# Second layer's first product by Strassen's algorithm, on two sets of tokens, in a three-stage float32 kernel

## The chip, the core and the metric

The kernel runs on one core of a Trainium2 chip. The metric is the time of one execution on the device in microseconds (us). The profile comes from one such execution. PE is TensorE, DVE VectorE, ACT ScalarE, POOL GpSimd, and SP issues the DMAs.

## The reference

```python
# attention without a score matrix: 4 batches x 8 heads, 576 tokens, 64 columns
q_s = exp(q - max(q)) / (sum + 1e-9)          # over a head's 64 columns
k_s = exp(k - max(k)) / (sum + 1e-9)          # over the 576 tokens
x = q_s @ (k_s^T @ v)                         # -> 2304 tokens x 512
# first layer, 2048 hidden units
h = x @ w_in
x = (h * clip(h + 3, 0, 6) / 6) @ w_out
# second layer, 4 experts of 1024 hidden units
for e in range(4):
    out += p[:, e:e+1] * (max(x @ w1[e], 0) @ w2[e])     # p normalised over e
```

All inputs are float32; the first layer's weights are taken in through the 64 bits of doubles.

## The kernel before

A product x @ w is made of float32r halves: x = H + L, and H.H + H.L + L.H are summed in PSUM. So each product of 128 x 128 weights with some columns is three matmuls.

Attention comes first, batch by batch: `k_part`, `q_part` and `x_part`, which leaves x transposed (hidden units on partitions) as `xh` and `xl`. The first layer's weights are converted on DVE, ACT and POOL meanwhile (`w_half`, lines 455 to 492), half a chunk at a time.

Both layers work by steps (`h_part`, `y_part`): a chunk of 128 hidden units for a block of tokens. A step is 12 matmuls of the first product (lines 514 to 516: four parts of 128 inputs, three halves each), the nonlinearity with the split into `gh` and `gl`, and 12 matmuls of the second product (line 590). The first layer has 16 chunks in five passes over its six blocks of 256 to 448 tokens (`PASSES1`); after a pass a block's sum is evicted into `acc`, and after the last it is halved again into `xh` and `xl` (lines 637 and 639). The second layer has 32 chunks, four to a pass, over four blocks of 512 tokens and one of 256. Its nonlinearity is a Relu on ACT out of PSUM (line 559) and the rest `gl` on DVE, which reads PSUM once and SBUF once (line 562). Its second product has tokens on partitions, so each of its matmuls has 512 columns, and the eviction (line 650) weighs it with the expert's share.

The order of all engines' instructions is set by `Plan.order`, a list schedule with a table of costs and places (`w`: weight chunks, 6 and 2 more after the attention; `g`, `ph`, `r`). Each engine then works through its list in order, and only semaphores time it.

Of the kernel before, what the change touches and what calls it, by code (L numbers as in the profile page):

```python
# [22 lines left out]
E = 4  # L23
# [22 lines left out]

# the first load's start, and until when the tensor engine runs at half its clock
FIRST, COLD = 1.65, 30.0


def hop(a, b):
    """From the end of a part on one engine to the start of one that waits for it on another."""
    return 0.27 if b == "PE" else 0.2 if a == "PE" else 1.05 if a == "SP" else 0.16


class Op:
# [3 lines left out]
    __slots__ = ("eng", "fn", "deps", "key", "take", "give", "start", "end", "place", "on", "n",  # L60
                 "left", "at", "then", "due")
# [698 lines left out]
```

## Time and profile before

| | us |
|---|---|
| median of 3 runs | 1307.83 |
| lowest, highest | 1307.62, 1310.25 |
| the profiled execution, its span | 1307.6 |
| PE busy in it | 1268.7 |
| DVE, ACT, POOL busy | 503.2, 360.8, 248.0 |

The span runs from the first to the last instruction. A matmul's shown duration reaches over its successors, so PE's spacing is read from start times. "Idle before" is an engine's idle time in front of a group, with what ended it.

### The profile page before, as it was taken

The page shows a single profiled execution, that of the slowest core. Times are in us where ns is not written, and L with a number is a line of the kernel's source. Part 1 is how long each engine was busy: PE and PEld are TensorE (multiplying, and loading weights), DVE is VectorE, ACT ScalarE, POOL GpSimd, SP SyncE. Part 2 cuts the span into 40 slices and gives each one's busy share as a digit, 9 for nine tenths or more (in the row PEclk, how much of TensorE's full clock was granted, in tenths as well). Part 3 has the DMA queues.
Part 4 walks back from the last instruction along what each step waited for, and adds up shares of the span by engine and source line. Part 5 has one row for each costly group of instructions (what it writes and reads, how often), then busy time and mean ns, then how long its engine had stood idle before and what let it go on. Part 6 is the DMA issues. An engine that isn't in the chain of part 4 may idle for free.

```text
span 1307.6 us, 15363 instructions
## 1 busy us (share of the span) xinstructions
PE 1268.7 (97%) x6336; PEld 1101.3 (84%) x6336; DVE 503.2 (38%) x849; ACT 360.8 (28%) x680; POOL 248.0 (19%) x207
## 2 busy tenths in 40 slices
PE   4889999999999999999999999999999999999998
PEld 3778999899999999888888888888888888888887
DVE  8998641884345332222222222122222222222222
ACT  5676533552234334012112112102112112111111
POOL 4665132430005215003003003003003003000000
PEclk9998999999999999999999999999999999999999
DMA  8444120231003002002002002002001001000011
GB/s 283 120 136 124 48 66 1 65 98 33 1 1 97 1 1 65 1 1 65 1 1 65 1 1 65 1 1 65 1 1 63 3 1 33 1 1 1 33 45 68
DMA packets 19254, 54.02 MB, mean 41 GB/s; under 512 B 2288, under 2 KB 2288, under 8 KB 19184
## 3 DMA queue, kind: packets, MB, share of 16 engines
q1 hardware_dynamic: 19184, 53.04, 12.9%
q8 instruction: 50, 0.82, 0.3%
q14 instruction: 20, 0.16, 0.0%
HBM read 48.31 MB, written 4.72 MB: 41 GB/s over the span
## 4 chain that ended last, share of the span: by engine, by line
PE 76%; issue 11%; DVE 5%; POOL 3%; DMA 3%; ACT 1%; SPq 0%; DVEq 0%; POOLq 0%; ACTq 0%
PE y L590 37%; PE ph L514 12%; PE ph L516 12%; PE ph L515 12%; DMA raw<-in_w_dram 2%; POOL wt L468 1%; POOL wl L436 1%; DVE wt L476 1%; PE pa L407 1%; DVE raw L485 1%; DVE wt L471 1%; PE pa L310 0%; DVE qm L381 0%; DVE raw L479 0%; PE pa L303 0%
## 5 line engine op out<-in xcount | busy, mean ns | idle before, releaser
L514 PE MATMUL ph<-xh,wh 128*128 128x512 f32 (+4 forms) x1024 | 368.4, 360 | 0.5 <-ACT xh L414 0.5
L516 PE MATMUL ph<-xh,wl 128*128 128x512 f32 (+4 forms) x1024 | 366.1, 358 | 0.0
L515 PE MATMUL ph<-xl,wh 128*128 128x512 f32 (+4 forms) x1024 | 365.3, 357 | 0.8 <-DVE xl L416 0.7
L562 DVE SCALAR_TENSOR_TENSOR gl<-ph,gh 128x512 fp32r<-128x512 f32 (+1 forms) x160 | 102.1, 638 | 568.9 <-ACT gh L559 568.9
L559 ACT ACTIVATE gh<-ph 128x512 fp32r<-128x512 f32 (+1 forms) x160 | 89.2, 557 | 641.9 <-PE ph L516 615.3
L590 PE MATMUL y<-wh,gh 128*128 128x512 f32 x576 | 227.3, 395 | 0.0
L590 PE MATMUL y<-wl,gh 128*128 128x512 f32 x576 | 226.2, 393 | 0.0
L515 PEld LDWEIGHTS ph<-xl,wh 128*128 128x128 f32 x1024 | 192.8, 188 | 26.1 <-DVE xl L416 1.4
L514 PEld LDWEIGHTS ph<-xh,wh 128*128 128x128 f32 x1024 | 192.9, 188 | 25.3 <-ACT xh L414 1.5
L516 PEld LDWEIGHTS ph<-xh,wl 128*128 128x128 f32 x1024 | 192.8, 188 | 24.6
L436 POOL TENSOR_TENSOR wl<-raw,wh 128x512 fp32r<-128x512 f32 x64 | 81.5, 1294 | 539.0 <-ACT wh L449 538.9
L590 PE MATMUL y<-wh,gl 128*128 128x512 f32 x576 | 157.9, 391 | 0.0
L590 PE MATMUL y<-gh,wh 128*128 128x448 f32 (+3 forms) x384 | 132.8, 352 | 3.9 <-ACT gh L545 3.2
L590 PEld LDWEIGHTS y<-wh,gl 128*128 128x128 f32 x576 | 108.2, 188 | 25.4
L590 PEld LDWEIGHTS y<-wl,gh 128*128 128x128 f32 x576 | 108.0, 187 | 23.5
L590 PEld LDWEIGHTS y<-wh,gh 128*128 128x128 f32 x576 | 108.2, 188 | 23.0
L590 PE MATMUL y<-gh,wl 128*128 128x448 f32 (+3 forms) x384 | 127.5, 338 | 0.0
L539 DVE SCALAR_TENSOR_TENSOR r<-r,ph 128x448 f32<-128x448 f32 (+3 forms) x96 | 52.9, 551 | 140.8 <-ACT r L536 140.6
L650 DVE SCALAR_TENSOR_TENSOR acc<-y,pt,acc 128x512 f32<-128x512 f32 x126 | 86.2, 745 | 26.4 <-PE y L590 26.4
L536 ACT ACTIVATE r<-ph,three 128x448 f32<-128x448 f32 (+3 forms) x96 | 55.4, 577 | 134.4 <-PE ph L516 133.4
L590 PE MATMUL y<-gl,wh 128*128 128x448 f32 (+3 forms) x384 | 86.9, 344 | 0.0
L590 PEld LDWEIGHTS y<-gh,wh 128*128 128x128 f32 x384 | 72.6, 189 | 9.2 <-ACT gh L545 5.0
(85 smaller groups left out, 949.3 us busy)
## 6 DMA issues: line engine op xcount, KB each, us to landing
raw<-in_w_dram SPq DMA_DIRECT2D x62, 512.0 KB, 3.7
acc<-in_kt_dram SPq DMA_DIRECT2D x16, 288.0 KB, 3.8
out_dram<-acc SPq DMA_DIRECT2D x18, 256.0 KB, 2.1
vs<-in_v_dram SPq DMA_DIRECT2D x12, 322.5 KB, 4.3
qs<-in_q_dram SPq DMA_DIRECT2D x13, 256.0 KB, 3.7
acc<-in_v_dram SPq DMA_DIRECT2D x4, 322.5 KB, 5.5
acc<-in_w_dram SPq DMA_DIRECT2D x2, 512.0 KB, 7.6
acc<-in_q_dram SPq DMA_DIRECT2D x3, 256.0 KB, 3.9
```

Source lines behind the costliest of these rows:

```text
L407: nc.tensor.matmul(ps[o], lhsT=bd[j], rhs=qt[:, j, s0:s0 + n], start=True, stop=True)
L436: on(o).tensor_tensor(out=wl[c][:, cols], in0=x, in1=wh[c][:, cols].bitcast(F32), op=ALU.subtract)
L468: on(o).tensor_tensor(out=t(F32), in0=word(1, F32), in1=t(F32), op=ALU.mult)
L514: nc.tensor.matmul(ps[0], lhsT=hi, rhs=a, start=(k == 0), stop=False)
L515: nc.tensor.matmul(ps[0], lhsT=hi, rhs=b, start=False, stop=False)
L516: nc.tensor.matmul(ps[0], lhsT=lo, rhs=a, start=False, stop=(k == NK - 1))
L536: nc.scalar.activation(out=ps["r"], in_=ps[0], func=AF.Relu, bias=three)
L539: nc.vector.scalar_tensor_tensor(out=ps["r"], in0=ps["r"], scalar=6.0, in1=ps[0], op0=ALU.min, op1=ALU.mult)
L559: nc.scalar.activation(out=s["g"][0], in_=ps[0], func=AF.Relu)
L562: nc.vector.scalar_tensor_tensor(out=s["g"][1], in0=ps[0], scalar=0.0, in1=s["g"][0].bitcast(F32), op0=ALU.max, op1=ALU.subtract)
L590: nc.tensor.matmul(y, lhsT=l, rhs=r, start=(s["start"] and not low and m == 0), stop=(s["stop"] and bool(low)))
L650: o1 = add({"DVE": 0.62}, lambda o: nc.vector.scalar_tensor_tensor(out=a, in0=ybank[b], scalar=g, in1=a, op0=ALU.mult, op1=ALU.add), [made ...
```

## The change

**The second layer's first product** takes two chunks (a pair, 256 hidden units) and a unit of tokens at once. The units (`UNITS`) are 512, 512, 512 and 768 tokens, each cut into two halves of n = 256, 256, 256 and 384. Hidden units, inputs and tokens are each split in two, and Strassen's algorithm in Winograd's form makes the four blocks from seven products of half size instead of eight. Each product is 6 matmuls of n columns, 42 a round where there were 48. Products 6, 4 and 3 accumulate in the bank of 1, 7 and 5 after ACT has evicted these; DVE and POOL add up the blocks, ACT and DVE halve them into g (`h_ops`).

**x and the weights are formed as sums and differences.** `x_forms` makes seven operands of a unit out of `acc` and halves each. `w_first` does the same for the pair's weights, on POOL, DVE and ACT.

**Two sets of tokens.** Set 0 is units 0 and 1, set 1 units 2 and 3; all 16 pairs go over set 0 first. In set 0 each formed weight is stored to DRAM (`wd`, `vd`), in set 1 it is loaded from there. Pairs go in groups of two; the second product of a group (`y_ops`) runs as a head of two tiles, and the others lie between the products of the next round.

**The first layer** goes over blocks of 256 and 384 tokens, in passes of 3, 3, 6, 5 and 5 chunks. Weight places are now 24 and 2 more of 512 columns (half a chunk's H or L).

```diff
-# (first token, tokens) of the blocks that a pass over some hidden units goes through
-BLOCKS1 = [(0, 256), (256, 320), (576, 448), (1024, 448), (1472, 416), (1888, 416)]
-BLOCKS2 = [(0, 512), (512, 512), (1024, 512), (1536, 512), (2048, 256)]
-# (chunks from, to, blocks), one after the other
-PASSES1 = [(0, 3, (0, 1, 2)), (3, 6, (0, 1, 2)), (0, 6, (3, 4, 5)),
-           (6, 12, range(6)), (12, 16, range(6))]
+BLOCKS1 = [(0, 256), (256, 256), (512, 256), (768, 256), (1024, 256), (1280, 256), (1536, 384),
+           (1920, 384)]
+PASSES1 = [(0, 3, range(4)), (3, 6, range(4)), (0, 6, range(4, 8)), (6, 11, range(8)),
+           (11, 16, range(8))]
...
+UNITS = [(0, 256), (512, 256), (1024, 256), (1536, 384)]
+BLOCKS = [(0, 1), (2, 3)]
+HALVES = ((0, 0), (0, 1), (1, 0), (1, 1))
+FORM = {(0, 0): 1, (0, 1): 2, (1, 1): 4, (1, 0): 7}
+ORDER = (1, 7, 5, 6, 4, 3, 2)
+BANK = {1: 0, 6: 0, 7: 1, 4: 1, 5: 2, 3: 2, 2: 3}
+NPE = F2 // (2 * P)
+NW, NG, NT_ = 24, 2, 3
+MORE_W, MORE_G, MORE_T = 2, 4, 5
...
-    xl = big.tile([P, NK, NT], F32R, name="xl")
+    big, xp, wp, gp, tp, wsp = (pool(x) for x in ("big", "xp", "wp", "gp", "tp", "wsp"))
+    dram = pool("dram", space=bass.MemoryType.DRAM)
...
+        def summed(i, a, b, op):
+            def make(o):
+                o.place_tile = XT[o.place] if late_ else g_tile(o.place, F32)
+                tt(o, vals[i](), vals[a](), vals[b](), op)
+            o = temps[i] = add(either(2 * n), make, ready[a] + ready[b],
...
+        got = {}
+        if blk:
+            for i in ORDER:
+                pl = w_new(w1, (pr, i))
+                ld = load("sp", {"SP": 0.9}, lambda o, i=i: nc.sync.dma_start(
+                    out=w1[pr, i].bitcast(F32), in_=wd[pr, i - 1]), [pl, w_stored[pr, i]])
+                got[i] = ld, pl, []
+            return got
+        p0, p1 = [raw2(2 * pr + f, 0) for f in range(2)]
...
+        def form(i):
+            pl = w_new(w1, (pr, i))
+            o1 = add({"ACT": act(half)}, lambda o: nc.scalar.activation(
+                out=w1[pr, i][:, :half], in_=vals[i](), func=AF.Copy), ready[i] + [pl])
+            give = [("wtmp", temps[i])] if i in temps else []
+            o2 = add(rather_pool(half), lambda o: half_sub(
+                o, w1[pr, i][:, half:], vals[i](), w1[pr, i][:, :half]),
+                [o1] + (readers[i] if i in temps else []), None, give)
+            st = add({"SP": 0.9}, lambda o: nc.sync.dma_start(
+                out=wd[pr, i - 1], in_=w1[pr, i].bitcast(F32)), [o2])
+            w_stored[pr, i] = st
+            lows[i] = o2
...
+        def product(o, i):
+            (xh, xl), ww = xf[u, i], w1[pr, i]
+            opens = i in (1, 7, 5, 2)
+            for k in range(2):
+                hi, lo = ww[:, k * P:(k + 1) * P], ww[:, (2 + k) * P:(3 + k) * P]
+                a, b = xh[:, k * n:(k + 1) * n], xl[:, k * n:(k + 1) * n]
+                for m, (l, r) in enumerate(((hi, a), (lo, a), (hi, b))):
+                    nc.tensor.matmul(
+                        bank(i), lhsT=l, rhs=r, start=(opens and k == 0 and m == 0),
+                        stop=(k == 1 and m == 2), skip_group_check=not opens)
...
+        def evict(i):
+            def f(o, t):
+                nc.scalar.activation(out=t, in_=bank(i), func=AF.Copy)
+            return tmp({"ACT": act(n)}, f, [ops[i]])
...
+        def make(i):
+            deps = [weights[i][0], xf["op", (u, i)]]
+            deps += bank_free.get(BANK[i], [])
...
+                    o, y0.place_tile[:, :n], y0.place_tile[:, :n], u2.place_tile[:, :n], ALU.add),
+                    [s, u2])
+                blocks[1, 1] = y0, [pos["c22"]]
+            if i == 4:
+                u2 = pos["u2"]
+                c = tmp({"DVE": dve(n)}, lambda o, t: tt(
+                    o, t, bank(4), u2.place_tile[:, :n], ALU.add), [ops[4], u2])
+                bank_free[1] = [c]
+                pos["c21"] = c
...
+                add({"": 0.0}, lambda o: None, [c, pos["c21"], pos["c22"]], None, [("t", u2)])
+            if i == 2:
+                a0 = pos["a0"]
+                c = add({"DVE": dve(n)}, lambda o: tt(
+                    o, a0.place_tile[:, :n], bank(2), a0.place_tile[:, :n], ALU.add), [ops[2], a0])
...
+            def low(o):
+                g = made[key][0]
+                nc.vector.scalar_tensor_tensor(
+                    out=g[:, n:2 * n], in0=x(), scalar=0.0, in1=g[:, :n].bitcast(F32),
+                    op0=ALU.max, op1=ALU.subtract)
...
+        head = [part(0, 0, None), part(1, 0, None), part(0, 1, 0), part(1, 1, 0),
+                part(0, 1, 1), part(1, 1, 1)]
...
+                for x, pr in enumerate(group):
+                    make, made = h_ops(pr, u, weights[pr], step["last"])
+                    todo = [lambda i=i: make(i) for i in ORDER]
+                    while todo or (x == 0 and tail):
+                        if todo:
+                            todo.pop(0)()
+                        if x == 0:
...
+                head, rest = y_ops(u, group, gs, seconds, step)
+                for f in head:
+                    f()
+                tail = rest
```

On PE a step of the second layer before, here a part of one with `ph` the first product's bank and `y` the second's:

```order
L514 MATMUL ph1_117<-xh_82,wh23_4504 128x512
L590 MATMUL y0_5120<-wh22_4467,gh_5155 128x512
L590 MATMUL y0_5120<-wl22_4468,gh_5155 128x512
L590 MATMUL y1_5126<-wh22_4467,gh_5155 128x512
L590 MATMUL y1_5126<-wl22_4468,gh_5155 128x512
```

And after the change, the seven products of one round (`ps0` to `ps3` are their banks, `ps4` the second product's):

```order
L878 MATMUL ps0_111<-x010_4173,w_15_1_8364 128x256 x6
L878 MATMUL ps1_112<-x070_4318,w_15_7_8376 128x256 x6
L878 MATMUL ps2_113<-x050_4332,w_15_5_8389 128x256 x6
L878 MATMUL ps0_111<-x060_4340,w_15_6_8402 128x256 x6
L878 MATMUL ps1_112<-x040_4358,w_15_4_8415 128x256 x6
L878 MATMUL ps2_113<-x030_4401,w_15_3_8428 128x256 x6
L878 MATMUL ps3_114<-x020_4425,w_15_2_8440 128x256 x6
L1001 MATMUL ps4_115<-w_14_0_0_8452,g_8665 128x512
```

Twelve wide matmuls into one bank have become seven groups of six into four banks, and three banks are taken twice within a round.

On DVE, the second layer before had a rest per step and a block's evictions:

```order
L562 SCALAR_TENSOR_TENSOR gl_5424<-ph2_1594,gh_5423 128x512
L562 SCALAR_TENSOR_TENSOR gl_5452<-ph1_117,gh_5451 128x512
L650 SCALAR_TENSOR_TENSOR acc_84<-y0_5361,pt_85,acc_84 128x512
L650 SCALAR_TENSOR_TENSOR acc_84<-y1_5367,pt_85,acc_84 128x512
L650 SCALAR_TENSOR_TENSOR acc_84<-y2_5371,pt_85,acc_84 128x512
```

Now a round in set 0 stands there so (line 294 adds, 963 makes the rests; `t` and `g` lie in SBUF):

```order
L294 TENSOR_TENSOR t_7741<-t_7741,t_7750 128x256
L294 TENSOR_TENSOR t_7741<-t_7741,t_7761 128x256
L294 TENSOR_TENSOR t_7772<-ps1_112,t_7761 128x256
L294 TENSOR_TENSOR t_7784<-ps2_113,t_7761 128x256
L963 SCALAR_TENSOR_TENSOR g_7781<-t_7741,g_7781 128x256
L294 TENSOR_TENSOR t_7728<-ps3_114,t_7728 128x256
L963 SCALAR_TENSOR_TENSOR g_7786<-t_7772,g_7786 128x256
L963 SCALAR_TENSOR_TENSOR gx1_5245<-t_7784,gx1_5245 128x256
L963 SCALAR_TENSOR_TENSOR gx1_5245<-t_7728,gx1_5245 128x256
```

One operation per step has become nine per round, six of them with both operands in SBUF.

On DVE at the first gate (539) of the fourth pass, in block 0, the kernel before had these rows (436 is the last step of a weight's conversion, 471 and 476 are a short and a long one):

```order
L436 TENSOR_TENSOR wl10_2232<-wt1_115,wh10_2231 128x512
L539 SCALAR_TENSOR_TENSOR r_2325<-r_2325,ph0_116 128x256
L471 TENSOR_SCALAR wt0_114<-raw0_112 128x512
L548 TENSOR_TENSOR gl_2336<-r_2325,gh_2335 128x256
L630 TENSOR_SCALAR acc_84<-y0_2110 128x416
L630 TENSOR_SCALAR acc_84<-y2_2118 128x416
L476 SCALAR_TENSOR_TENSOR wt0_114<-raw0_112,wt0_114 128x512
```

After the change the same place (gate 615, short step 543, long step 549):

```order
L615 SCALAR_TENSOR_TENSOR r_2517<-r_2517,ps0_111 128x256
L294 TENSOR_TENSOR w_8_1_1_2424<-st0_109,w_8_1_0_2423 128x512
L682 TENSOR_SCALAR acc_81<-ps4_115 128x384
L682 TENSOR_SCALAR acc_81<-ps6_117 128x384
L294 TENSOR_TENSOR g_2533<-r_2517,g_2533 128x256
L543 TENSOR_SCALAR st0_109<-st1_110 128x512
L615 SCALAR_TENSOR_TENSOR r_2563<-r_2563,ps2_113 128x256
L543 TENSOR_SCALAR st1_110<-st0_109 128x512
L294 TENSOR_TENSOR g_2590<-r_2563,g_2590 128x256
L549 SCALAR_TENSOR_TENSOR st0_109<-st1_110,st0_109 128x512
```

Half of chunk 10 was in place before that gate; now the second half of chunk 8 comes behind it, and chunks 9 and 10 between the later gates.

## Rows read from the trace of the kernel before

**Rows 1.** The page's head and its line on PE (busy us, share of the span, instructions).
```profile
span 1307.6 us, 15363 instructions
PE 1268.7 (97%) x6336; PEld 1101.3 (84%) x6336; DVE 503.2 (38%) x849; ACT 360.8 (28%) x680; POOL 248.0 (19%) x207
```

**Rows 2.** Stretches: us; busy of PE, PEld, DVE, ACT, POOL; granted clock; DMA share; GB/s.
```profile
30.00:65.00 35.00, 30.29 (x184) 25.77 (x185) 34.12 (x67) 24.39 (x56) 24.48 (x21) 0.89 0.44 130
600.00:700.00 100.00, 100.00 (x459) 82.50 (x458) 24.90 (x38) 16.05 (x29) 10.48 (x9) 1.00 0.07 22
```

**Rows 3.** PE in order of time: start us, us, line, operation; 512 columns, then 256.
```profile
519.43 0.40 PE L514 MATMUL ph<-xh,wh 128*128 128x512 f32 x1
547.09 0.40 PE L514 MATMUL ph<-xh,wh 128*128 128x512 f32 x1
...
117.64 0.28 PE L514 MATMUL ph<-xh,wh 128*128 128x256 f32 x1
118.94 0.28 PE L516 MATMUL ph<-xh,wl 128*128 128x256 f32 x1
```

**Rows 4.** The same view, first and last of a run: 320, 448, 416 columns.
```profile
126.23 0.31 PE L514 MATMUL ph<-xh,wh 128*128 128x320 f32 x1
127.84 0.31 PE L516 MATMUL ph<-xh,wl 128*128 128x320 f32 x1
...
146.27 0.36 PE L514 MATMUL ph<-xh,wh 128*128 128x448 f32 x1
147.67 0.36 PE L515 MATMUL ph<-xl,wh 128*128 128x448 f32 x1
...
485.37 0.35 PE L514 MATMUL ph<-xh,wh 128*128 128x416 f32 x1
494.37 0.35 PE L514 MATMUL ph<-xh,wh 128*128 128x416 f32 x1
```

**Rows 5.** Groups of DVE instructions by shape: busy us, mean ns, idle before.
```profile
L562 DVE SCALAR_TENSOR_TENSOR gl<-ph,gh 128x512 fp32r<-128x512 f32 x128 | 88.5, 692 | 505.7 <-ACT gh L559 505.7
L562 DVE SCALAR_TENSOR_TENSOR gl<-ph,gh 128x256 fp32r<-128x256 f32 x32 | 13.5, 423 | 63.3 <-ACT gh L559 63.3
L650 DVE SCALAR_TENSOR_TENSOR acc<-y,pt,acc 128x512 f32<-128x512 f32 x126 | 86.2, 745 | 26.4 <-PE y L590 26.4
L476 DVE SCALAR_TENSOR_TENSOR wt<-raw,wt 128x512 int32<-128x512 int32 x30 | 28.3, 943 | 1.5 <-ACT wt L474 1.2
L471 DVE TENSOR_SCALAR wt<-raw 128x512 int32<-128x512 int32 x30 | 16.9, 575 | 8.2 <-DMA raw<-in_w_dram 7.5 <-POOL wl L436 0.6
L436 DVE TENSOR_TENSOR wl<-wt,wh 128x512 fp32r<-128x512 f32 x12 | 16.3, 1356 | 4.7 <-ACT wh L489 4.2 <-PE y L590 0.5
```

**Rows 6.** Groups of ACT and of POOL instructions by shape, the same columns.
```profile
L559 ACT ACTIVATE gh<-ph 128x256 fp32r<-128x256 f32 x32 | 12.3, 384 | 71.3 <-PE ph L516 44.7 <-DVE acc L650 26.5
...
L639 POOL TENSOR_TENSOR xl<-acc,xh 128x256 fp32r<-128x256 f32 x4 | 3.1, 802 | 9.9 <-ACT xh L637 9.9
```

**Rows 7.** All engines in order of time near the end: a product's end to ACT.
```profile
1300.55 0.39 PE L590 MATMUL y<-wh,gh 128*128 128x512 f32 x1
1300.75 0.38 ACT L559 ACTIVATE gh<-ph 128x256 fp32r<-128x256 f32 x1 [2.42 <-PE ph L516]
```

**Rows 8.** All engines in order of time around 248 us.
```profile
247.28 0.69 DVE L485 SCALAR_TENSOR_TENSOR raw<-raw 128x512 f32<-128x512 uint32 x1
248.05 1.29 POOL L468 TENSOR_TENSOR wt<-raw,wt 128x512 f32<-128x512 f32 x1 [2.76 <-DVE raw L485]
248.13 1.76 DVE L485 SCALAR_TENSOR_TENSOR raw<-raw 128x512 f32<-128x512 uint32 x1 [0.16 <-ACT raw L482]
```

**Rows 9.** In order of time at the fourth pass's start: PE's wait, a DVE step.
```profile
251.02 0.45 PE L590 MATMUL y<-gh,wh 128*128 128x416 f32 x1 [2.66 <-ACT gh L545]
...
253.67 0.42 DVE L471 TENSOR_SCALAR wt<-raw 128x512 int32<-128x512 int32 x1
```

**Rows 10.** DMA issues: KB each, median us to landing.
```profile
out_dram<-acc SPq DMA_DIRECT2D x18, 256.0 KB, 2.1
```

More of the change, by code (lines that the diff above doesn't have):

```diff
@@ L280, in pa @@
     def pa(o, width):
[L281 to L283 removed]
+        return PS[2 + o.place][:, :width]
     def pa_place(early):
@@ L518, in h_part @@
-        if s["layer"] == 1:
-            deps = x_done[s["bi"]] if s["first"] else []
-        else:
-            deps = [o for (a, m), o in y_made.items() if a < t0 + n and a + m > t0]
-            deps = [x for o in deps for x in o]
-        o0 = add({"PE": 12 * pe}, product, deps + w_done[c][:1] + h_before, ("ph", None),
+                hi, lo = (w0[c, 0, x][:, k * P:(k + 1) * P] for x in range(2))
+                x = x0[bi, k // 2]
+                a = x[:, (k % 2) * n:(k % 2 + 1) * n]
+                b = x[:, (2 + k % 2) * n:(3 + k % 2) * n]
@@ L524, in h_part @@
+                nc.tensor.matmul(pst[0], lhsT=hi, rhs=a, start=(k == 0), stop=False)
+                nc.tensor.matmul(pst[0], lhsT=hi, rhs=b, start=False, stop=False)
+                nc.tensor.matmul(pst[0], lhsT=lo, rhs=a, start=False, stop=(k == NK - 1))
+        deps = x_done[bi] if s["first"] else []
+        o0 = add({"PE": 12 * pe(n)}, product, deps + w_done[c][:1] + h_before, ("ph", None),
                  key=i - 1.0, due=s["due"])
         h_before[:] = [o0]
-        def new_g(o):
-            pl = gp if o.place < 2 else late["wp"]
-            s["g"] = [pl.tile([P, 512], F32R, tag=f"g{x}{o.place}", name=f"g{x}")[:, :n]
-                      for x in "hl"]
@@ new lines, in h_part, with clip, gate, high @@
+        if s["x_last"]:
+            kind = "x4" if n <= 256 else "x6"
+            o0.give += [(kind, x0_place[bi, k]) for k in range(2)]
+        def clip(o):
+            pst["r"] = t_tile(o, "r")[:, :n]
+            nc.scalar.activation(out=pst["r"], in_=pst[0], func=AF.Relu, bias=three)
+        def gate(o):
+            nc.vector.scalar_tensor_tensor(
+                out=pst["r"], in0=pst["r"], scalar=6.0, in1=pst[0], op0=ALU.min, op1=ALU.mult)
+        def high(o):
+            g = g_tile(o.place)
+            s["g"] = [g[:, :n], g[:, n:2 * n]]
+            nc.scalar.activation(out=s["g"][0], in_=pst["r"], func=AF.Copy)
@@ new lines, in h_part @@
+        o1 = add({"ACT": act(n) + 0.06}, clip, [o0], ("t", None), key=MAIN + i)
+        o2 = add({"DVE": dve(n)}, gate, [o1], None, [("ph", o0)], key=MAIN + i)
+        o3 = add({"ACT": act(n)}, high, [o2], ("g", None), key=MAIN + i)
+        o4 = add({"Pool": pool_(n), "DVE": dve(n)} if s["first"] else {"DVE": dve(n)},
+                 lambda o: half_sub(o, s["g"][1], pst["r"], s["g"][0]), [o3], None, [("t", o1)],
+                 key=MAIN + i)
+        if i >= len(steps) - 4:
+            last1.append(o2)
@@ L594, in y_part @@
         for low in range(2):
-            for b in range(parts):
+            for b in range(NK):
                 deps = [o4 if low else o3, w_done[c][1]]
@@ L669, in normal @@
             )
-        norm.append(add({"DVE": 0.7}, normal, [ld]))
-    def more_places(o):
-        att.close()
-        late["wp"] = pool("wp2")
-        late["ph"] = pool("ps_h2", space=PSUM).tile([P, 512], F32, name="ph2")
+        norm.append(add({"DVE": 1.0}, normal, [ld]))
     for b in range(B):
@@ L691, in tile_kernel, with more_g, make @@
     for i, s in enumerate(steps):
         h_part(i, s)
+    for b in range(NK):
+        add({"": 0.0}, lambda o: None, [evicted[b]], None, [("y", b)])
+    for i in range(4):
+        bank_free[i] = list(last1)
+    add({"": 0.0}, lambda o: None, stage_ops, None,
+        [("raw2", i) for i in range(4)] + [("wtmp", i) for i in range(4)])
+    for u in BLOCKS[0]:
+        x_forms(u)
+    def more_g(first, new):
+        def make(o):
+            t = new(o)
+            g_more[first], g_more[first + 1] = t[:, :768], t[:, 768:]
+        return make
@@ L694, in tile_kernel @@
+    for f in tail:
+        f()
     with tc.manual_schedule():
```

765 lines of the change are left out of this document (513 added, 252 removed).

## The prediction

> **What bounds the kernel now.** I read the page first: PE is busy for 1268.7 of 1307.6 us, POOL for 248.0 and DVE for 503.2 [rows 1]. A share over the whole span hides stages, so next came the table of stretches. Between 600 and 700 us PE has no idle time at a granted clock of 1.00, the 2.4 GHz level, while DVE is busy for 25 us and POOL for 10. Between 30 and 65 us it is DVE that is full, 34.1 of 35 us, and PE is busy for 30.3 [rows 2]. So attention is bound by DVE, and what follows by the number of matmuls times their spacing.
>
> The spacing is read from start times, since the durations of neighbours overlap. 120 matmuls of 512 columns take 27.66 us, 0.2305 each; 11 of 256 take 1.30 us, 0.1182 [rows 3]. At 320, 448 and 416 columns it is 1.61/11 = 0.1464, 1.40/7 = 0.2000 and 9.00/48 = 0.1875 [rows 4]. A column costs nearly the same at every width, so narrow matmuls lose little, and fewer columns are fewer microseconds. No row has 384 columns. Two thirds of the way from 320 to 416 gives 0.1738; the cost per column at 512 would give 0.1729, that at 256 0.1773. I take 0.1738, between its nearest neighbours.
>
> The profiled execution's span is its whole time, 0.2 us below the median of the three runs; the sum below starts from 1307.6. A measurement of this kernel can tell about 0.2%, 2.6 us, from no change.
>
> **The change, part by part.** The second layer's first product had 32 chunks x 12 matmuls over four blocks of 512 and one of 256: 384 x (4 x 0.2305 + 0.1182) = 399.4 us. Now 16 pairs of chunks take 7 x 6 = 42 matmuls in each unit, three units at 256 and one at 384: 672 x (3 x 0.1182 + 0.1738) = 355.1 us. That is **-44.3**.
>
> The first layer runs 16 chunks x 24 matmuls over its blocks. Before, one such matmul in each of the six blocks cost 0.1182 + 0.1464 + 2 x 0.2000 + 2 x 0.1875 = 1.0396; in the eight new blocks it is 6 x 0.1182 + 2 x 0.1738 = 1.0568. Times 384 that is **+6.6**. The bounds of the 384-column price move both parts together, 1440 matmuls: -1.3 to +5.0.
>
> The second product stays at 16 x 18 x 6 = 1728 matmuls of 512 columns: 0.
>
> Attention: before its last matmul PE now has 539 first-layer matmuls in its order, 63.6 us of them at these spacings; it had 384, 57.3 us. DVE, the bound there, has 23 gates instead of 17 and narrower rests, 24 instead of 32 (wider) x parts. With a fixed 0.154 us and 1.05 ns a column (from 0.423 and 0.692 [rows 5]) that is about 3 us more of DVE for 6 us more of PE work. I take **0**, between -4 and +4.
>
> Fourth pass: a chunk's weights need places that the third pass frees only in its last block. There were 8 chunk places, two of them ahead; now 26 places, each for the H or the L of a half chunk, hold six chunks and one half. In DVE's order the conversion of chunks 8 to 10 now stands between the pass's own gates, two chunks later than before. From the first gate of that pass to the sixth I count 4 and 3 of the two short conversion steps, 4 and 3 of the two long ones, two 512-column operations in SBUF, five gates, five rests and two 384-column evictions. At the mean prices 0.575, 0.943, 1.356, 0.42 and 0.56 [rows 5] that is 18.6 us; at undisturbed ones, 0.42 for a short step [rows 9] and 0.69 for the others, 14.5; against 5 x 24 x 0.1182 = 14.2 us of PE. Before, PE lost 2.66 us at this place, waiting for ACT in DVE's chain [rows 9]. The sixth chunk in that pass is gone, which helps the next change of pass. I take **+4**, nearer to the mean prices, between 0 and +9.
>
> Forming x for units 0 and 1 (22 DVE or POOL operations of 512 columns, 0.69 to 1.36 us, and 14 on ACT) costs nothing: unit 0 is ready 30 steps before the first layer ends, 20 x 24 x 0.1182 + 10 x 24 x 0.1738 = 98 us, and the cover for unit 1 is still some 75. If that cover went, the 15 to 30 us would stand on PE's path. The former halving of x by ACT and POOL falls away, and was hidden as well.
>
> Between the sets, units 2 and 3 are formed while products run. Unit 3's seven operands of 768 columns need places that come back only behind unit 1's last tiles, and four places for g come back only behind them, while the second pair of unit 2 already needs two of these. That is 11 operations of some 0.96 us (the line above at 768), half of them beside 21 us of PE work. **+3**, between 0 and +8.
>
> Weights: in set 0 each pair has 11 POOL operations of 256 columns at 0.802 [rows 6] and two of 512 at 1.29 [rows 8], 11.4 us, under 21 us of PE (two rounds of 42 x 0.1182 + 24 x 0.2305 = 10.5). Its 11 stores and 4 loads on SP move 15 x 256 KB; one landed in 2.1 us [rows 10]. Set 1 reloads 22 tiles per group, whose 52 us and at least 6 us of lead cover them: 0, if each landing stays under 6 us.
>
> In a round a bank that took one product is evicted before the next accumulates on it. ACT starts 0.20 us after the slot of the last matmul ends [rows 7], runs 0.384 [rows 6], and a handover back costs about as much, 0.8 us in all; two products, 1.42 us, lie between. An ACT copy of a weight in front (0.38 to 0.6) uses that up. 16 groups with some 0.1 to 0.3 us at a few places: **+4**, between 0 and +15.
>
> **The sum:** 1307.6 - 44.3 + 6.6 + 0 + 4 + 3 + 4 = 1280.9, so **1281 us**. At the end the last tile alone is evicted (0.745 [rows 5]) and stored, as before.
>
> **A rule that speaks against it.** In set 0 DVE and POOL now work on SBUF at the same time. Of nine short DVE operations in a round, six read two operands from SBUF (the four rests, two sums); before, a rest in this layer read one from PSUM. A row shows what such an operation risks: one that takes 0.69 us alone took 1.76 when it began 0.08 us after a POOL operation of 1.29 us [rows 8]. The Trainium skill, SBUF — State Buffer, section Who interferes with whom, says that a DVE instruction with two SBUF inputs and a GpSimd instruction that reads SBUF exclude each other for the whole instruction. By that rule, the trace agrees: 0.69 + 1.07 is DVE waiting to POOL's end.
>
> The price: let such an operation take t. In a unit of set 0 DVE must do 3 x 0.42 + 6t while PE runs the second pair's seven products (4.96 us), and then 0.42 + 4t before PE has run 20 second-layer matmuls (4.6 us), with 0.2 for the handover. The lateness is 10t - 7.7 us a unit. Alone t = 0.42. POOL is busy for 11.4 of 21 us, so a mean hold of 0.54 x 0.40 (half of 0.802) gives t = 0.64: still nothing late. Held every time, t = 1.2: 4.3 us x 16 units = 69 us.
>
> **The rivals.** *Small waits in every round:* ACT's weight copies and DVE's queue make each of 32 rounds in set 0 lose 0.7 us instead of a tenth; 1281 - 4 + 23 = 1300. For it: seven products a round wait for a bank, and two engines that work in order hand the banks over. Against: DVE's nine short operations and its evictions are 9 x 0.42 + 2 x 0.745 = 5.3 us of a round of 10.5, ACT's eight 3.1, and a bank has two products of room.
>
> *DVE held by POOL, slower:* the same place, priced above. It ends behind the kernel before once the lateness is over 1.9 us a unit (30 us / 16), t = 0.96, that is two holds in three. At t = 1.0 it is 37 us: 1277 + 37 = 1314. For it: the planner's list puts both engines' operations back to back there, and the means of 0.943 and 1.356 [rows 5] show holds to be common. Against: POOL's operations are mostly 0.8 us, and most DVE operations wait for PE's products, not for each other.
>
> *The gain doesn't arrive:* DVE, full in attention, and the fewer places for weights cost 22 us more before the second layer, 1303. Little speaks for it, as the order gives PE more to do there, not less.
>
> **How the numbers follow.** The first forecast has 0.74, from 1267 to 1293: with the added 11 us gone it would be 1269.9, with attention's 4 and the cheap 384 columns 1264.6, of which I leave out the last. Upwards, 12 us are half of what the upper bounds add (5 + 4 + 5 + 5 + 11 = 30). The others: small waits 0.10; DVE held 0.10, of which a tenth or so stays under 1303; the lost gain 0.06. The range 1267 to 1303 holds the first and second case. Faster by over 0.2%: 0.74 + 0.09 + 0.03 = 0.86. Within 0.2%: 0.03. Slower: 0.11, nearly all of it DVE held by POOL.
>
> **What would show it.** Right: matmuls of 256 columns at 0.118 us spacing in the second layer, some 753 us (355 + 398) plus under 10 for it, a granted clock of 1.00 there, idle PE only at the starts of the fourth and fifth pass and between the sets. DVE groups of 256 columns with two SBUF inputs between 0.42 and 0.7 us. Wrong: PE waits for DVE's rests in every unit of set 0 (the third case), for ACT's evictions in every round (the second), for loads in set 1, or a 384-column spacing over 0.178.

## The result, and the profile after

| us | before | after |
|---|---|---|
| median | 1308.41 | 1269.82 |
| lowest, highest | 1307.62, 1310.25 | 1268.65, 1270.20 |
| the profiled execution's span | 1307.6 | 1267.6 |

The ratio is 0.9703 with an interval of 0.9689 to 0.9716: faster, 11 us below the forecast and inside its range, near the low end. After's profiled execution took 1269.44 us, 1.8 more than its span, and every execution with both numbers shows some 1.7 to 2.0 us outside the span. So the span of 1307.6 us that the forecast started from was not the whole time, as the prediction took it to be; spans are compared with spans below.

The head and the first lines of the page after, which answer to [rows 1]:

```profile
span 1267.6 us, 20591 instructions
PE 1229.7 (97%) x7896; PEld 1148.6 (91%) x7896; DVE 727.8 (57%) x1367; ACT 511.5 (40%) x1178; POOL 338.7 (27%) x347
```

PE is 39 us less busy, while DVE gained 225 us, ACT 151 and POOL 91, and PE's share is still 97%. The table of stretches, the columns as in [rows 2]: the two of before, then the attention, the rest of the first layer, the first set and the second.

```profile
30.00:65.00 35.00, 29.00 (x216) 26.95 (x216) 31.07 (x64) 24.20 (x55) 25.79 (x23) 0.95 0.38 114
600.00:700.00 100.00, 100.00 (x621) 90.32 (x620) 61.76 (x103) 40.91 (x114) 52.52 (x61) 1.00 0.50 175
...
0.00:155.00 155.00, 127.04 (x943) 119.38 (x943) 130.47 (x266) 100.87 (x218) 82.46 (x78) 0.96 0.47 150
155.00:520.00 365.00, 358.90 (x2624) 356.67 (x2623) 197.07 (x381) 155.91 (x327) 89.63 (x86) 1.00 0.15 50
520.00:840.00 320.00, 319.88 (x1999) 289.46 (x1998) 205.96 (x346) 137.41 (x374) 163.15 (x182) 1.00 0.54 187
840.00:1268.00 428.00, 423.92 (x2335) 383.09 (x2333) 194.32 (x376) 117.27 (x261) 3.42 (x2) 1.00 0.33 106
```

In the second layer PE has next to no idle time: it is busy for 319.88 of 320 us in the first set beside DVE at 206 and POOL at 163, and for 423.92 of 428 in the second, of which the last 4 are the final eviction and store. So there the added work of the other engines does not stand on the path. In order of time on PE (start us, us): a run of 384 columns, the one width that no row of before had, with the matmul behind it; the second layer's first and last matmuls; and, from its middle, a run of 256 columns and one of 512 with what follows.

```profile
501.34 2.24 PE L642 MATMUL ps<-g,w 128*128 128x384 f32 x12
503.42 0.33 PE L598 MATMUL ps<-x,w 128*128 128x384 f32 x1
...
509.71 10.23 PE L878 MATMUL ps<-x,w 128*128 128x256 f32 x84
...
1006.01 7.36 PE L878 MATMUL ps<-x,w 128*128 128x256 f32 x60
1013.21 2.91 PE L1001 MATMUL ps<-w,g 128*128 128x512 f32 x12
1015.96 2.88 PE L1001 MATMUL ps<-w,gs 128*128 128x512 f32 x12
...
1255.60 8.32 PE L1001 MATMUL ps<-w,gs 128*128 128x512 f32 x36
```

12 matmuls of 384 columns take 2.08 us, 0.1733 each. 60 of 256 columns take 7.20 us, 0.1200 each, where before had 0.1182; 12 of 512 take 2.75 us, 0.2292 each, where before had 0.2305. The second layer runs from 509.71 to about 1263.9 (the last 36 at 0.2305): 754.2 us. Most of what PE lost between 155 us and there stands at the start of the fourth pass, where [rows 9] showed 2.66 us; the longest waits:

```profile
248.98 1.94 PE L642 MATMUL ps<-g,w 128*128 128x256 f32 x12 [1.02 <-ACT r L612]
257.94 0.38 PE L642 MATMUL ps<-g,w 128*128 128x256 f32 x1 [1.26 <-ACT w L563]
259.85 1.58 PE L642 MATMUL ps<-g,w 128*128 128x256 f32 x11 [1.53 <-DVE w L294]
276.00 4.25 PE L642 MATMUL ps<-g,w 128*128 128x256 f32 x31 [1.62 <-DVE acc L684]
```

Last, groups of the first set by shape (520 to 840 us; busy us, mean ns, idle before), against [rows 5] and [rows 6]:

```profile
L963 DVE SCALAR_TENSOR_TENSOR gx<-t,gx 128x256 fp32r<-128x256 f32 x62 | 42.5, 697 | 1.8 <-ACT gx L956 1.7
L963 DVE SCALAR_TENSOR_TENSOR g<-t,g 128x256 fp32r<-128x256 f32 x62 | 40.9, 669 | 0.2 <-ACT g L956 0.2
L294 DVE TENSOR_TENSOR t<-t 128x256 f32<-128x256 f32 x53 | 38.1, 718 | 14.0 <-ACT t L886 12.4
L294 DVE TENSOR_TENSOR t<-ps,t 128x256 f32<-128x256 f32 x91 | 36.3, 415 | 4.6 <-PE ps L878 4.2 <-ACT w L795 0.3
L294 POOL TENSOR_TENSOR w<-st,w 128x256 fp32r<-128x256 f32 x96 | 79.2, 839 | 76.5 <-ACT w L795 76.5
```

DVE's operations on two SBUF operands take 0.67 to 0.72 us beside POOL. The mean of these three groups is 0.69. With one operand from PSUM they take 0.415, and in the second set, where POOL has two instructions in all, the rests of 256 columns are at 0.42 again.

### The profile page after: what moved, and what is told of

It reads as the page before. It is cut to its first block, busy times and chain, and to the rows that moved or that the text cites. A ratio compares the mean times of both kernels' runs of the same rounds, so it can differ in the third digit from the quotient of the medians.

```text
span 1267.6 us, 20591 instructions
## 1 busy us (share of the span) xinstructions
PE 1229.7 (97%) x7896; PEld 1148.6 (91%) x7896; DVE 727.8 (57%) x1367; ACT 511.5 (40%) x1178; POOL 338.7 (27%) x347
## 4 chain that ended last, share of the span: by engine, by line
PE 82%; DVE 3%; DMA 2%; POOL 1%; issue 1%; ACT 1%; SPq 0%; POOLq 0%; DVEq 0%; ACTq 0%
PE ps L1001 30%; PE ps L878 27%; PE ps L642 12%; PE ps L600 4%; PE ps L599 4%; PE ps L598 4%; DMA st<-in_w_dram 1%; POOL w L294 1%; POOL st L294 1%; DVE st L558 0%; DVE st L549 0%; DVE g L294 0%; PE ps L485 0%; DMA qs<-in_q_dram 0%; DVE r L615 0%
## 5 line engine op out<-in xcount | busy, mean ns | idle before, releaser
L878 PEld LDWEIGHTS ps<-x,w 128*128 128x128 f32 x2688 | 370.6, 190 | 8.7 <-ACT t L886 0.3
L878 PE MATMUL ps<-x,w 128*128 128x256 f32 (+1 forms) x2688 | 376.2, 296 | 0.1
L886 ACT ACTIVATE t<-ps 128x256 f32<-128x256 f32 (+1 forms) x256 | 104.9, 411 | 382.9 <-PE ps L878 381.3
L642 PE MATMUL ps<-g,w 128*128 128x256 f32 (+1 forms) x1536 | 233.3, 299 | 8.3 <-DVE acc L684 1.6
L1001 PE MATMUL ps<-w,g 128*128 128x512 f32 x960 | 233.6, 391 | 0.0
L642 PEld LDWEIGHTS ps<-g,w 128*128 128x128 f32 x1536 | 213.3, 190 | 11.8 <-DVE acc L684 1.8
L294 POOL TENSOR_TENSOR w<-st,w 128x256 fp32r<-128x256 f32 (+1 forms) x157 | 151.0, 981 | 236.9 <-ACT w L563 93.3
L1001 PEld LDWEIGHTS ps<-w,g 128*128 128x128 f32 x960 | 178.0, 188 | 35.0
L599 PE MATMUL ps<-x,w 128*128 128x256 f32 (+1 forms) x512 | 152.3, 297 | 3.3 <-DVE x L496 3.3
L598 PE MATMUL ps<-x,w 128*128 128x256 f32 (+1 forms) x512 | 153.0, 299 | 0.0
L600 PE MATMUL ps<-x,w 128*128 128x256 f32 (+1 forms) x512 | 152.1, 297 | 0.0
L599 PEld LDWEIGHTS ps<-x,w 128*128 128x128 f32 x512 | 98.5, 192 | 3.6 <-DVE x L496 3.5
L598 PEld LDWEIGHTS ps<-x,w 128*128 128x128 f32 x512 | 98.5, 192 | 0.4
L600 PEld LDWEIGHTS ps<-x,w 128*128 128x128 f32 x512 | 98.4, 192 | 0.0
L1001 PE MATMUL ps<-w,gx 128*128 128x512 f32 x384 | 95.9, 392 | 0.0
L1001 PE MATMUL ps<-w,gs 128*128 128x512 f32 x384 | 92.5, 390 | 0.0
```

The lines of the kernel that those rows point to most:

```text
L294: on(o).tensor_tensor(out=out, in0=a, in1=b, op=op)
L598: nc.tensor.matmul(pst[0], lhsT=hi, rhs=a, start=(k == 0), stop=False)
L599: nc.tensor.matmul(pst[0], lhsT=hi, rhs=b, start=False, stop=False)
L600: nc.tensor.matmul(pst[0], lhsT=lo, rhs=a, start=False, stop=(k == NK - 1))
L642: nc.tensor.matmul(y, lhsT=l, rhs=r, start=(s["start"] and not low and m == 0), stop=(s["stop"] and bool(low)))
L878: nc.tensor.matmul(bank(i), lhsT=l, rhs=r, start=(opens and k == 0 and m == 0), stop=(k == 1 and m == 2), skip_group_check=not opens)
```

## Experiments

Each ran beside the kernel before on the same chip. "+" and "-" are differences of spans, of one execution each and mostly from different chips. The ratios to the kernel before give the same within 2 us, but for one run that is named below.

**What the half products are worth**, by doing one of the seven twice:

```diff
-            for k in range(2):
+            for k in (0, 1, 0, 1) if i == 2 else (0, 1):
```

> The changed kernel with product 2 of every round done twice (the second run overwrites the first), so 48 matmuls a round as without Strassen. If the second layer is bound by matmuls times spacing alone: 6 x (3 x 0.1182 + 0.1754) x 16 = 50.9 us more, 1320.7. If other engines hide part of the eighth product behind waits that the seven have: under 45 us more.

The planner is told of the longer product. Median 1322.58, ratio to the kernel before 1.0100 (1.0086 to 1.0113); span 1320.6, **+53.0** against the changed kernel. By spacing the 384 added matmuls cost 16 x 6 x (3 x 0.1182 + 0.1733) = 50.7. So 384 matmuls fewer are worth at least what they cost, and with eight products the kernel is slower than before.

**The banks' cover**, by putting product 1, whose bank product 6 takes, right in front of it:

```diff
-ORDER = (1, 7, 5, 6, 4, 3, 2)
+ORDER = (7, 5, 1, 6, 4, 3, 2)
```

> The changed kernel with the products in the order 7, 5, 1, 6, 4, 3, 2, so that product 6 accumulates on the bank of product 1 with nothing between them. If a handover through ACT costs 0.20 + 0.384 + 0.2 us (0.49 in the middle at 384 columns) and was hidden by the two products between: 40 rounds x 0.78 + 16 x 0.89 = 45 us more, 1315; the 8 rounds with second-layer matmuls between lose nothing. If handovers are cheap by themselves, whatever the order: no change within 0.3%.

Median 1315.10, ratio 1.0048 (1.0034 to 1.0062); span 1310.9, **+43.3** (the profiled execution was the fastest of six; by medians it is 45.3); the second layer alone is 47 us longer. Waits of PE (us in total, times, longest) in the second layer, and one in order of time:

```profile
PE ps L878 <- ACT t L886: 32.6, 57, 0.8
...
604.77 3.13 PE L878 MATMUL ps<-x,w 128*128 128x256 f32 x24 [0.53 <-ACT t L886]
```

PE waits 57 times, about once in each of the 56 rounds in which nothing lies between the two products. A shown wait is shorter than the true one, since the shown matmul in front of it (0.28 us [rows 3]) reaches past its slot of 0.12: 0.53 is 0.69 by start times. By start times these waits are 0.70 us on average at 256 columns and 0.81 at 384, 42 of the 47 us together; the other 5 are not traced. The prediction had put the handover at 0.8 for 256 columns. With two products between, nothing of it is left.

**Late rests**, by writing each rest of the second layer twice:

```diff
-                nc.vector.scalar_tensor_tensor(
-                    out=g[:, n:2 * n], in0=x(), scalar=0.0, in1=g[:, :n].bitcast(F32),
+                for _ in range(2):
+                    nc.vector.scalar_tensor_tensor(
+                        out=g[:, n:2 * n], in0=x(), scalar=0.0, in1=g[:, :n].bitcast(F32),
```

> The changed kernel with each rest of the second layer made twice by DVE, the order otherwise unchanged. By the lateness formula with t = 0.6 in set 0: (3 x 0.42 + 10 x 0.6 - 4.96) + (0.42 + 8 x 0.6 + 0.2 - 4.6) = 3.1 us a unit, 50 us over 16 units, nothing in set 1: 1320, with PE waiting for DVE behind each second round of set 0. If only DVE's busy share matters (13 short operations and evictions, 8.9 of 10.5 us): no change within 0.3%.

Median 1318.33, ratio 1.0069 (1.0055 to 1.0083); span 1316.8, **+49.2**. Waits of PE in the second layer:

```profile
PE ps L1002 <- ACT gx L956: 19.8, 15, 2.1
PE ps L1002 <- DVE gx L964: 13.5, 9, 1.7
PE ps L1002 <- DVE g L964: 3.1, 7, 1.0
```

All are at the second product's start, where the formula put them, and about its 50 us came. That it came so close is in part luck. The formula's t stands for operations with two SBUF operands, and the 0.60 was a mean over all short operations. In this run's first set the groups are these (520 to 840 us; busy us, mean ns, idle before):

```profile
L964 DVE SCALAR_TENSOR_TENSOR gx<-t,gx 128x256 fp32r<-128x256 f32 x106 | 67.9, 646 | 1.8
L964 DVE SCALAR_TENSOR_TENSOR g<-t,g 128x256 fp32r<-128x256 f32 x106 | 64.6, 614 | 1.8
L294 DVE TENSOR_TENSOR t<-t 128x256 f32<-128x256 f32 x48 | 32.3, 673 | 9.6 <-ACT t L886 7.8 <-DVE t L294 0.5
```

Their mean is t = 0.64, and with it the formula, 18t - 7.7 us a unit, gives 61 us. So it has the place right and the size within a quarter. For the changed kernel, with t = 0.69, it leaves 0.8 us of room a unit: enough, and not much.

**POOL's cover**, by writing seven of a pair's POOL operations twice, without a word to the planner:

```diff
-            o2 = add(rather_pool(half), lambda o: half_sub(
-                o, w1[pr, i][:, half:], vals[i](), w1[pr, i][:, :half]),
+            o2 = add(rather_pool(half), lambda o: [half_sub(
+                o, w1[pr, i][:, half:], vals[i](), w1[pr, i][:, :half]) for _ in range(2)],
```

> The changed kernel with the subtraction of each of the seven weight forms of a pair written twice on POOL (same values, same order), 7 x .83 = 5.8 us more of POOL in 21 us, so that it is busy .82 of the first set in place of .54. A mean DVE instruction there takes .60 with POOL at .54, .42 alone; by the same proportion .69 at .82. Theory (the prediction's lateness, 10t - 7.7, stays below zero up to t = .77): no wait of TensorE on DVE or ScalarE, within 3 us of 1267.6. Rival (VectorE held by POOL, as the prediction's slower case had it): TensorE waits at the second product's start in the first set, 15 us or more. A wait for weights themselves (w from POOL, L878) would be a third thing: POOL's own rate.

Median 1315.89, ratio 1.0058 (1.0045 to 1.0072); span 1313.0, **+45.4**, 43 of it in the second layer. The theory fell, and the rival named the wrong place for nearly all of it. One stretch, and the waits of PE in the second layer:

```profile
600.00:700.00 100.00, 91.88 (x545) 81.61 (x544) 58.33 (x92) 36.34 (x100) 68.99 (x84) 0.97 0.46 162
663.00:666.40 3.40, 3.03 (x14) 3.03 (x15) 1.34 (x4) 1.42 (x5) 3.24 (x5) 0.50 0.01 4
...
PE ps L878 <- ACT t L886: 25.0, 12, 3.1
PE ps L1001 <- ACT gx L956: 2.7, 6, 0.5
```

POOL is not full (0.69 and not 0.82, as the set grew longer), and the second product's start waits for 2.7 us only. PE waits for ACT's eviction of a bank, 2.9 to 3.1 us, once in 48 us. These waits do not make up the 43 us by themselves. At six of these seven waits the granted clock fell to 0.50, the 1.2 GHz level, for a stretch that reached beyond the wait, as from 663.0 to 666.4 us: 14 matmuls began there, where 28 would at 0.12 us each. Such stretches sum to 27 us in the second layer, and by the matmuls that began in them some 13 of the 43 us went there. Of the lists of ACT, POOL and PE in order of time around one such wait, the rows that lead to it:

```profile
662.63 0.42 ACT L795 ACTIVATE w<-st 128x256 fp32r<-128x256 f32 x1 [4.11 <-POOL st L294]
662.95 0.37 ACT L886 ACTIVATE t<-ps 128x256 f32<-128x256 f32 x1
...
661.87 2.50 POOL L294 TENSOR_TENSOR st<-st 128x256 f32<-128x256 f32 x3 [7.12 <-DMA st<-in_w_dram]
...
663.37 5.19 PE L878 MATMUL ps<-x,w 128*128 128x256 f32 x30 [2.93 <-ACT t L886]
```

POOL's first sum for a new pair waited for raw rows, and by the code the places for these come free only when POOL is through with an earlier pair. On ACT the rounding of that sum (L795) stands ahead of the bank's eviction (L886), and PE pays. In the changed kernel POOL waits for raw rows just as long without harm:

```profile
677.77 0.74 POOL L294 TENSOR_TENSOR st<-st 128x256 f32<-128x256 f32 x1 [7.29 <-DMA st<-in_w_dram]
```

ACT reaches L795 there with no wait for POOL at all. Telling the planner of the doubled work separates order from rate:

```diff
-            o2 = add(rather_pool(half), lambda o: [half_sub(
+            o2 = add({"Pool": 2 * pool_(half)}, lambda o: [half_sub(
```

> The run before (each subtraction of a first product's weight form twice on POOL) with one more edit: the planner is told the double price and that POOL alone does it, so that it orders the instructions of all engines anew and gives some of POOL's other work to VectorE. There TensorE waited in every second pair of chunks, since an eviction of a bank on ScalarE stood behind a rounding that waited for POOL's sum (4.1 us), which waited for a raw load (7.1 us). Theory (an order made at the wrong price, not POOL's rate: .7 busy is not full): most of the 45 us goes, 1268 to 1285. Rival (at this load POOL itself, or VectorE held by it, is the limit): 1300 or more, with waits at the second product's start or for weights.

Median 1293.82, ratio 0.9871 (0.9855 to 0.9888); span 1294.5, **+26.9** against the changed kernel, between the two bands. This is the run where the ratios tell another size: 0.9871 for 0.9703 is 22 us, as the chip was slower (the kernel before took 1310.59 there) and the profiled execution the slowest of four. Waits in the first set:

```profile
PE ps L878 <- ACT t L886: 13.9, 6, 2.8
...
ACT w L795 <- DVE st L294: 23.7, 12, 4.0
DVE st L294 <- DMA st<-in_w_dram: 28.9, 5, 6.5
```

So 40% of the loss by spans, and half of it by the ratios, was the order. The rest has the same chain with DVE in POOL's place, since the sums moved there, and it still begins with raw rows; here too the granted clock was at 0.50 for 3.4 us behind three of the six waits. Whether more places for raw rows would end it wasn't tried.

**Transfers**, by issuing each store of a weight form twice:

```diff
-            st = add({"SP": 0.9}, lambda o: nc.sync.dma_start(
-                out=wd[pr, i - 1], in_=w1[pr, i].bitcast(F32)), [o2])
+            for _ in range(2):
+                st = add({"SP": 0.9}, lambda o: nc.sync.dma_start(
+                    out=wd[pr, i - 1], in_=w1[pr, i].bitcast(F32)), [o2])
```

> The changed kernel with every store of a first set's weight form issued twice to the same place, so that about 29 MB more are moved in the first set's 300 us. The DMA engines' busy share there was .50 to .57. Theory (stores and loads cost nothing, since no TensorE wait ends at a transfer): no change, within 2 us of 1267.6, with the share at .7 to .85. Rival (the transfers are near their limit, and loads that come later hold the weight forms): raw rows land late, TensorE waits for forms in the first set, 10 us or more and over 1278.

Median 1269.71, ratio 0.9698 (0.9685 to 0.9711); span 1268.4, **+0.8**: no change, with 29.4 MB more. The stretch of 600 to 700 us and the landing times:

```profile
600.00:700.00 100.00, 99.32 (x614) 89.25 (x613) 60.72 (x104) 40.87 (x114) 52.17 (x61) 1.00 0.76 273
...
wd<-w SPq DMA_DIRECT2D x224, 256.0 KB, 3.2
w<-wd SPq DMA_DIRECT2D x112, 256.0 KB, 3.0
```

**The first layer.** Five runs divide what happened before 510 us. First the new blocks alone in the kernel before, with the passes and parts of x that go with them. Then the changed kernel with one head pair to a part of the attention's output: the change also puts two head pairs in one bank where they fit and evicts them together ("pairing").

```diff
-BLOCKS1 = [(0, 256), (256, 320), (576, 448), (1024, 448), (1472, 416), (1888, 416)]
+BLOCKS1 = [(0, 256), (256, 256), (512, 256), (768, 256), (1024, 256), (1280, 256), (1536, 384),
+           (1920, 384)]
```

> The kernel before with only the first layer's blocks, passes and x parts of the changed one; its second layer, places and cost table stay. Spacing theory: 384 first-layer matmuls per set of blocks at 0.1182 x 6 + 0.1754 x 2 = 1.060 us for 1.0396, so 7.8 us more, and some 2 us more waiting at the fourth pass. If attention's 6 us in the changed kernel come from the narrower blocks and x parts, the time is some 4 us over before (1312); if they come from the pairing of heads, the places or the cost table, it is 8 to 10 us over (1317).

```diff
-        js = [(0, 1), (2, 3)] if 2 * n <= 512 else [(0,), (1,), (2,), (3,)]
+        js = [(0,), (1,), (2,), (3,)]
```

> The changed kernel with the attention's output taken per head pair, as before, and no longer two head pairs in one bank, evicted by one instruction each on ScalarE and VectorE: 44 such parts for 24, so 20 more evictions and 20 more subtractions of the same columns in all. With the new blocks alone the kernel before took 8 us longer, so the stretch with the attention gained some 14 us from something else. Theory (the pairing is what gave it, a VectorE and ScalarE instruction's fixed part of about .15 to .2 us times 20 on each, and fewer handovers): 4 to 14 us longer, 1271 to 1282. Rival (not the pairing but the order of the parts, which follows from the new cost table and the places): within 2 us of 1267.6.

Blocks: median 1317.50, ratio 1.0061 (1.0049 to 1.0074); span 1316.6, **+9.0** against before, of which the first layer's narrower matmuls explain 6.6; so the attention's gain is not theirs. One head pair: median 1272.16, ratio 0.9718 (0.9705 to 0.9731); span 1271.2, **+3.6** against after, just below the band for pairing and above the rival's. By the ratios it is 2 us, and the two intervals overlap, so the whole time hardly tells it from no change; the attention alone does, as said below.

The diff also raises the planner's costs for the attention's parts and the weight conversion, mostly by 0.04 to 0.25 us each and towards the measured means ([rows 5] has 0.575 for a step priced at 0.34 and now at 0.58). In the changed kernel these were put back. In the kernel before they were put in, together with the new costs of its nonlinearities and evictions, without and with the new blocks; one line of some twenty:

```diff
-        o2 = add({"ACT": 0.67}, lambda o: nc.scalar.activation(
+        o2 = add({"ACT": 0.77}, lambda o: nc.scalar.activation(
```

> The changed kernel with the costs that its planner takes for the parts of the attention, of the x parts and of the conversion of the first layer's weights put back to the smaller numbers of the kernel before (so only the order of these parts moves, not an instruction). Theory (the order from the new costs gave the stretch with the attention its gain): 4 to 14 us longer, 1271 to 1282, with TensorE waits in the first 155 us. Rival (the pairing of head pairs, or the larger number of places, gave it): within 2 us of 1267.6.

> The kernel before with the planner's costs of the changed kernel for the parts of the attention, the first layer's weights and the evictions (no instruction, block or place differs; only the order). Putting the old costs of these parts back into the changed kernel took 8.7 us. Theory (what the costs give belongs to the attention, which both kernels share): 1298 to 1303, so that part of the measured gain has nothing to do with the half products. Rival (they give something only together with the new blocks, pairs and places): within 2 us of 1307.6, or slower.

> The kernel before with the new blocks (1316.6 by themselves) and with the changed kernel's costs. Theory (the costs mend the stretch with the attention in the new blocks as well, by 8 to 9 us): 1306 to 1309; what is then left to the attention of the changed kernel is the pairing (3.6 us by the run with one head pair) and its places. Rival (no effect without pairs and places): 1315 to 1318.

Old costs in the changed kernel: median 1278.26, ratio 0.9767 (0.9753 to 0.9780); span 1276.3, **+8.7**. New costs in the kernel before: 1302.55, 0.9955 (0.9941 to 0.9968); span 1300.6, **-7.0**. With the new blocks too: 1307.35, 0.9994 (0.9985 to 1.0003); span 1306.0, **-10.6** against the blocks alone. So an order made with truer prices is worth 7 to 11 us in all three (6 to 9 by the ratios), with the same instructions; a few of them change engine, as POOL's 207 in the kernel before become 200. From the tables of stretches, 240 to 300 us of before and of before with the new costs, where PE's losses at the fourth pass went:

```profile
240.00:300.00 60.00, 56.60 (x376) 54.50 (x375) 50.14 (x86) 33.25 (x63) 22.67 (x17) 1.00 0.34 100
```

```profile
240.00:300.00 60.00, 59.40 (x395) 58.02 (x394) 47.92 (x84) 33.14 (x62) 19.54 (x15) 1.00 0.24 73
```

**The fourth pass's waits**, by cutting the third pass in two, so that the first three chunks' places come free sooner:

```diff
-PASSES1 = [(0, 3, range(4)), (3, 6, range(4)), (0, 6, range(4, 8)), (6, 11, range(8)),
+PASSES1 = [(0, 3, range(4)), (3, 6, range(4)), (0, 3, range(4, 8)), (3, 6, range(4, 8)), (6, 11, range(8)),
```

> The changed kernel with one line of PASSES1 different: the pass of the first layer over chunks 0 to 5 and the blocks behind the attention is cut in two, chunks 0 to 2 and then 3 to 5, so that three chunks' places come free about 35 us earlier and the conversion of the next weights can begin then. In the changed kernel TensorE waits there for weights: 1.02, 1.26, 1.53 and 1.62 us at 249 to 276 us and some shorter ones, 5.4 us or so. Theory (those waits come from places that free late): most of them go, 3 to 5 us less, span 1262.5 to 1264.5 against 1267.6. What it costs: one more sum per block and output tile in the accumulator, 4 blocks x 4 sums on VectorE, which has idle time there. Rival (the conversion's own length, VectorE and ScalarE beside the evictions, sets the waits, not the places): the waits move by 35 us and stay, 1267 to 1268.

Median **1262.02**, ratio 0.9646 (0.9633 to 0.9659); span 1260.1, **-7.5**: faster than both kernels. The stretches of 155 to 240 and 240 to 300 us:

```profile
155.00:240.00 85.00, 85.00 (x591) 85.00 (x591) 50.64 (x94) 40.47 (x82) 26.77 (x24) 1.00 0.13 44
240.00:300.00 60.00, 60.00 (x493) 59.95 (x492) 41.08 (x84) 27.72 (x57) 9.88 (x7) 1.00 0.15 54
```

DVE does the conversion from 155 us on (50.6 us there, 29.8 in the changed kernel), and PE waits nowhere in these 145 us, where it showed 5.4 us of waits. By start times that is 7.0 us: from the last attention matmuls to the second layer PE spent 12.6 us more than its first-layer matmuls at their spacings in the changed kernel, and 5.6 here. The last attention matmuls start 1.6 us earlier, at 153.8 us. The order moved there too, but that much shows nothing: in the seven traces whose order up to 160 us is the changed kernel's, they start between 153.2 and 155.7.

## Why the prediction was right, and where its terms were off

The sign, the mechanism and the range were right; the forecast was too long by 13.3 us of span.

- *The first product, -44.3:* right. 355.1 and 398.3 make 753.4; the second layer took 754.2. The eighth product cost 53.0, its matmuls and a little more. The 384-column spacing is 0.1733 for 0.1738. The 256-column one is 0.1200 and not 0.1182, some 3.6 us over 2016 matmuls, and the second product's 0.2292 for 0.2305 gave back some 2.2 of it; so that the layer came within 1 us is in part luck. Why the spacings moved is not shown.
- *The first layer, +6.6:* too small by the same spacing. Over its 2304 matmuls of 256 columns 0.0018 us make some 4 us.
- *Small waits at the banks, +4:* they are 0. In the second layer PE waits for nothing. The handover was right in size (0.70 for 0.8), and the two products between cover it wholly. The ACT copies in front did no harm in this order; once POOL was late, one of them held up an eviction, and 43 us were lost.
- *Between the sets, +3:* 0. PE is busy without a break from 840 us on.
- *Attention, 0:* this was the largest miss, about -6. PE's last attention matmuls start at 155.4 us (154.9 before), with 63.7 us of first-layer matmuls ahead of them instead of 57.3. The step that failed was to count DVE's instructions only, and not the order that they get from the cost table, which was in the diff. What took its place is read from the rows below the list.
- *Fourth pass, +4:* the waits sum to some 5.4 us for 3.4 before, so +2 as they are shown. Right in place and cause, as the split pass shows: with places free earlier the waits are gone.
- *Weights, x and DMAs at 0:* right, also with twice the stores. But the cover of the weights is thinner than "11.4 of 21 us" suggests: at 17 of 21 it was gone, through an ACT instruction that stood ahead of the eviction, with POOL busy for 0.69. About half of that loss went with an order made at the right price.
- *DVE held by POOL:* the holds came a little dearer than priced, t = 0.69 for 0.64, the mean of the three groups of the first set with two SBUF operands. 10 x 0.69 - 7.7 stays below zero. With POOL's subtractions doubled the same three groups took 0.79; the formula then gives 0.2 us a unit, some 3 us, and PE waited 2.7 us at the second product's start. The rival's condition, two holds in three or t = 0.96, was met in no run, so its price of 30 us and more is not tested.

The attention's -6 can be divided by the starts of PE's last attention matmuls. In three of the runs, blocks with new costs, one head pair and old costs, they are:

```profile
172.60 0.81 PE L408 MATMUL pa<-qt,bd 128*128 128x384 f32 x2
172.53 0.81 PE L485 MATMUL ps<-qt,bd 128*128 128x384 f32 x2
152.70 0.81 PE L485 MATMUL ps<-qt,bd 128*128 128x384 f32 x2
```

How many first-layer matmuls stand ahead of them differs by order, so these are taken off at the spacings of the prediction: 78.0, 77.8 and 54.4 us here. What is left of the start is 97.6 us before, 97.5 with the new blocks, 94.6 with blocks and new costs, 94.7 with one head pair, 98.3 with the old costs, and 91.7 in the changed kernel (89.5 to 92.0 in the seven traces with its order). So the costs gave some 3 us, by one trace on either side, and pairing some 3 more on top of them; with the old costs pairing gave nothing. The larger part of what the costs were worth in the kernel before, 5 us and more, came behind the attention.

The terms off, -4, -3, -6 and -2, make -15, and the first layer's spacing makes +4. That is -11 of the 13.3 us; the 2 us that are left are no more than what executions of one order differ by at the attention's end (153.2 to 155.7 us). The mechanism is shown by three runs: the eighth product, the neighbouring products and the split pass each moved what they were to move. How the first layer's parts add up in whole times is only rough: blocks with costs at 1306.0, less 44.3 and 3.6, would be 1258.1, and the changed kernel took 1267.6. After the split pass 1260.1 was reached.

## What to carry to other kernels

- Where PE is full, fewer matmuls are worth count times spacing, if each bank has two products between its use and its reuse: with none between it cost 0.70 us each time at 256 columns, with two nothing.
- A helper engine's share says little about its cover. Look at what stands behind its result in another engine's queue: POOL at 0.7 stopped PE through an ACT instruction that was only ahead of the eviction.
- In a kernel whose order comes from a cost table, the table is a part of the change: correcting prices moved 6 to 11 us with the instructions kept, and it should be tried alone, before the large edit.

## What the runs showed of the hardware

A hold shows in the changed kernel's rows of the first set, in order of time: a sum on two SBUF operands takes 0.43 us alone, and two of them take 1.54, 0.77 each, while POOL works on SBUF.

```profile
659.73 0.43 DVE L294 TENSOR_TENSOR t<-t 128x256 f32<-128x256 f32 x1 [0.44 <-ACT t L886]
...
664.40 5.21 POOL L294 TENSOR_TENSOR w<-st,w 128x256 fp32r<-128x256 f32 x5 [1.11 <-ACT w L795]
664.77 1.54 DVE L294 TENSOR_TENSOR t<-t 128x256 f32<-128x256 f32 x2 [0.53 <-ACT t L886]
```

POOL's five subtractions beside them take 1.04 us each, where one of this shape took 0.80 in [rows 6]. The prediction read [rows 8] as DVE waiting to POOL's end. That is a little too strict: DVE's operation there ended 0.55 us after POOL's, and it takes 0.69 alone.

I had not expected two things. Raising the DMA engines' share from 0.50 to 0.76 moved a store's landing only from 3.0 to 3.2 us. And with waits of 3 us on PE every 48 us the granted clock read 0.97 over 600 to 700 us, with 0.50 in the stretches at the waits, where it was 1.00 without them; the run that waited 0.7 us in most rounds kept 1.00.
